# Turning experts' rows on VectorE in squares of 32x32, a tile of row numbers for each group, and scatters three a pair of heads

## Chip, cores, metric

One core of one Trainium2 chip. The metric is device time of the whole program in microseconds (us), the median of several executions. Runs of one batch share a chip; the experiments make five batches on four chips, and the kernel before was run again in each of them.

## The reference

Attention with a selective bias, then a mixture of eight experts, of which each token uses one:

```python
# attention: 8 batches x 8 heads x 576 tokens x 64, float32
s_pos = np.maximum(s, 0.0); cum = np.cumsum(s_pos, axis=-1)
scores = np.where(causal, -1e9, scale * q @ k.T + np.minimum(-(cum_i - cum_j), 0.0))
x = softmax(scores) @ v                       # -> (8, 576, 512)
# experts, for every batch b and token s in order
fresh_e = argmax(x[b, s] @ w_gate)
e = fresh_e if s == 0 or local_gate[b, s] < 0.5 else prev_e
h = np.maximum(x[b, s] @ w1[e], 0.0)          # w1[e]: 512 x 1024
out[b, s] = p[e] * (h @ w2[e])                # w2[e]: 1024 x 512
```

## The kernel before

The kernel runs attention in 32 pairs of heads. Beside it, it sorts the tokens by expert: each group of batches yields row numbers (`slot_i`), with which GpSimd scatters token rows to `x_rows` in DRAM. The experts then work in units on blocks of 128 gathered rows: a *double* unit has two blocks, a *single* one, a *mixed* one two halves with different weights. Layer 1 reads the rows with the features on the partitions (`xT`), so each block of 128 rows x 512 features has to be turned, as four squares of 128x128. In the kernel before TensorE turns a square by one transpose into PSUM (273 ns long at the median, the four of a block 0.11 us apart) and VectorE copies the result (0.69 us a block):

```python
class Turned:
    def product(self, i, k, n, x, ps):
        ps = self.ps = ps.rearrange("p (c n) -> p c n", c=DK)                  # DK = 4
        for c in range(DK):
            self.nc.tensor.transpose(ps[:, c, :], x[:, ...], self.ident)      # L1070
        ...
    def copies(self, i, k, x):
        nc.vector.tensor_copy(self.xT[i][:, :, k * P : k * P + P], self.ps)    # L1078
        nc.vector.tensor_copy(self.at[i, k], x[:, XI : XI + 1])                # L1081
        nc.vector.tensor_copy(self.gate[i, k], x[:, XI + 1 :])                 # L1082
```

The blocks of unit i+2 are turned inside layer 2 of unit i. A pass of layer 2 is 16 matmuls of 128x512, about 7 us (6.87 from start to start, without transposes). Where unit i is single and unit i+2 double, one pass has to hide two blocks, and this happens seven times:

```python
    def layer2(i, k, then):
        for c in range(FK):                                    # FK = 8
            ... mm(ps, lhsT=hT[i][:, c, a : a + m], rhs=wn[:, c, :], ...)      # L1211
            if c in then:
                turn_x(*then[c])
        nc.vector.tensor_scalar_mul(y, ps, gate[i, k])
        ...
    def second(i):
        for k in range(nbs[i]):
            layer2(i, k, {3: (i + 2, k)} if nbs[i] == 2 else {1: (i + 2, 0), 5: (i + 2, 1)})
```

The sort has one tile of row numbers for all groups, and its steps are hung into the pairs of heads by a plan:

```python
        self.slot = self.t("slot_i", [P, M], I32)              # one tile, rewritten by each group
        nc.vector.tensor_copy(self.slot, slot)                 # L1003
        ...
            for f in g.scatters:                               # two scatters a pair
                place = max(place + 1, 2 * (n + 4))
                at(place // 2, 3 + place % 2, f)
        ...
        at(28, 1, fetch_early)                                 # rows of the first two units
```

## Time and profile before

| | kernel before |
|---|---|
| time, median of 3 (range) | 834.43 us (826.62 to 834.91) |
| profiled span | 828.1 us |
| until the first matmul of layer 1 | 262.4 us |
| the seven passes with two blocks, each with the layer 1 behind it | 150.9 us |
| VectorE busy | 213.0 us (26%) |

TensorE is 96% of the chain that ends last, and the waits behind the rest are all in attention. The span is that of one profiled execution; times are of executions of their own. In the profile PE is TensorE, DVE is VectorE, POOL is GpSimd, ACT is ScalarE and SP is SyncE. In a line of the timeline the columns are start, duration, engine, source line, operation, output and inputs, shapes, count, and in brackets the idle time ahead of it with what ended it.

### The profile page before, as it was taken

How to read it: one execution, taken by the hardware profiler on the slowest of the kernel's cores; microseconds unless marked ns; L12 is line 12 of the kernel's file. 1: busy time of each engine (PE TensorE's matmuls, PEld its weight loads, DVE VectorE, ACT ScalarE, POOL GpSimd, SP SyncE). 2: the span in 40 equal slices, each digit the busy share in tenths (PEclk: the TensorE clock that was granted, in tenths of full speed). 3: DMA queues.
4: the chain of work that ended last, by engine and by line, in shares of the span. 5: the costliest groups of instructions: out<-in, count | busy, mean ns of one | idle time of the engine just before them, and what ended most of it. 6: DMA issues, size and time to landing. Idle time of an engine off the chain costs nothing.

```text
span 828.1 us, 19789 instructions
## 1 busy us (share of the span) xinstructions
PE 805.7 (97%) x8153; PEld 603.5 (73%) x8153; DVE 213.0 (26%) x700; ACT 188.7 (23%) x535; POOL 174.5 (21%) x329
## 2 busy tenths in 40 slices
PE   9999999998989999998999989999999999999996
PEld 8989988897878856864777647776677766676762
DVE  2234533553434753111111111111111111111111
ACT  5767677665652100000000000000000000000000
POOL 3422254253541231010110102101111011010001
PEclk9999999998989999999999999999999999999998
DMA  9486589785555399964999459993699846995001
GB/s 316 156 283 195 167 299 330 243 254 196 161 206 210 99 329 406 395 198 166 327 393 358 125 192 333 389 365 118 223 341 396 332 135 235 345 407 181 20 15 42
DMA packets 64148, 204.56 MB, mean 247 GB/s; under 512 B 8269, under 2 KB 8301, under 8 KB 64048
## 3 DMA queue, kind: packets, MB, share of 16 engines
q1 hardware_dynamic: 55008, 172.41, 59.4%
q0 software_dynamic: 8896, 30.47, 9.8%
q8 instruction: 66, 1.08, 0.5%
q10 hardware_dynamic: 144, 0.33, 0.1%
q14 instruction: 34, 0.28, 0.1%
HBM read 179.93 MB, written 23.76 MB: 246 GB/s over the span
## 4 chain that ended last, share of the span: by engine, by line
PE 96%; issue 1%; ACT 1%; DMA 0%; POOL 0%; DVE 0%; POOLq 0%; DVEq 0%; ACTq 0%
PE yp L1211 32%; PE hp L1187 29%; PE o L407 13%; PE ps L329 11%; PE hp L1194 4%; PE o L369 2%; PE xp L1070 2%; PE o L285 1%; PE bank L963 1%; PE bank L941 1%; PE o L350 1%; ACT sc L338 0%; DMA x_rows<-x,r_slot_i 0%; PE bank L984 0%; POOL sc L344 0%
## 5 line engine op out<-in xcount | busy, mean ns | idle before, releaser
L1211 PE MATMUL yp<-w,hT 128*128 128x512 f32 (+1 forms) x528 | 221.1, 594 | 0.0
L1187 PE MATMUL hp<-xT,w 128*128 128x256 f32 (+1 forms) x1088 | 192.1, 337 | 0.0
L1187 PEld LDWEIGHTS hp<-xT,w 128*128 128x128 f32 x1088 | 172.1, 191 | 23.9 <-issue 7.8
L338 ACT ACTIVATE sc<-ps,bias 128x256 f32<-128x256 f32 (+3 forms) x448 | 156.6, 481 | 66.6 <-PE ps L329 64.7
L1211 PEld LDWEIGHTS yp<-w,hT 128*128 128x128 f32 (+1 forms) x528 | 88.0, 180 | 100.5 <-issue 99.5
L1202 ACT ACTIVATE hT<-hp 128x512 f32<-128x512 f32 x38 | 22.7, 597 | 505.6 <-PE hp L1187 421.7
L1218 POOL DMA_INDIRECT out_dram<-y,at_gate x38 | 38.4, 1011 | 459.3 <-DVE y L1217 444.4
L407 PE MATMUL o<-v,sc 128*64 128x74 f32 x3072 | 116.8, 232 | 3.5 <-POOL sc L344 3.4
L407 PEld LDWEIGHTS o<-v,sc 128*64 128x64 f32 x3072 | 111.7, 139 | 11.0 <-issue 5.9
L329 PE MATMUL ps<-q,k 64*128 64x320 f32 (+2 forms) x768 | 94.1, 392 | 0.0
L344 POOL TENSOR_SCALAR_AFFINE_SELECT sc<-sc 128x256 f32<-128x256 f32 x160 | 66.0, 419 | 129.4 <-issue 66.9
L1200 DVE TENSOR_SCALAR hT<-hp 128x512 f32<-128x512 f32 x38 | 26.2, 689 | 221.2 <-PE hp L1187 187.7
L329 PEld LDWEIGHTS ps<-q,k 64*128 64x128 f32 x768 | 70.4, 191 | 15.8 <-issue 0.8
L1211 PE MATMUL yp<-x,hT 128*128 128x512 f32 (+1 forms) x144 | 66.5, 608 | 0.0
L1217 DVE TENSOR_SCALAR y<-yp,at_gate 128x512 f32<-128x512 f32 x38 | 28.5, 750 | 135.6 <-PE yp L1211 135.6
L1187 PEld LDWEIGHTS hp<-xT,x 128*128 128x128 f32 x320 | 46.1, 191 | 5.8 <-issue 2.6
L1187 PE MATMUL hp<-xT,x 128*128 128x128 f32 (+1 forms) x320 | 50.1, 317 | 0.0
L1078 DVE COPY xT<-xp 128x512 f32<-128x512 f32 x36 | 24.9, 691 | 82.8 <-PE xp L1070 82.7
L1029 POOL DMA_INDIRECT x_rows<-x,r_slot_i x40 | 38.6, 966 | 16.0 <-DMA xg<-x_rows 7.5
L1211 PEld LDWEIGHTS yp<-x,hT 128*128 128x128 f32 (+1 forms) x144 | 25.2, 182 | 22.4 <-issue 22.1
L409 DVE RECIPROCAL recs<-o 128x4 f32<-128x4 f32 x64 | 12.1, 189 | 93.6 <-PE o L407 93.6
L412 DVE TENSOR_TENSOR x<-o,recs 128x292 f32<-128x292 f32 x64 | 34.4, 538 | 2.2
(160 smaller groups left out, 430.3 us busy)
## 6 DMA issues: line engine op xcount, KB each, us to landing
w<-in_w_dram SPq DMA_DIRECT2D x184, 512.0 KB, 8.2
x<-in_w_dram SPq DMA_DIRECT2D x56, 512.0 KB, 7.9
v<-in_vx_dram SPq DMA_DIRECT2D x32, 370.0 KB, 5.6
vt<-in_vz_dram SPq DMA_DIRECT2D x32, 320.0 KB, 3.4
k<-in_kz_dram SPq DMA_DIRECT2D x31, 320.0 KB, 4.9
q<-in_q_dram SPq DMA_DIRECT2D x32, 288.0 KB, 6.1
xg<-x_rows POOLq DMA_DIRECT2D x30, 293.0 KB, 8.4
x_rows<-r_empty SPq DMA_DIRECT2D x6, 293.0 KB, 4.7
```

What stands on the lines that cost most here:

```text
L329: mm(ps[:, h, at : at + z - a], lhsT=kb[d, c * P : c * P + P], rhs=qb[d, a:z], start=True, stop=True)
L338: nc.scalar.activation(scs[n, u][:, h, at : at + z - a], raw[u][:, h, at : at + z - a], Act.Exp, bias=bias[:, i : i + 1], scale=scale)
L344: nc.gpsimd.affine_select(out=x, in_=x, compare_op=Alu.is_ge, fill=0.0, base=0, pattern=[[0, 2], [1, P]], channel_multiplier=-1)
L407: mm(y, lhsT=w, rhs=x, start=start, stop=stop)
L412: nc.vector.tensor_tensor(x, y, rec.unsqueeze(3).to_broadcast([P, t1 - t0, 2, HW]), op=Alu.mult)
L1029: self.s.nc.gpsimd.indirect_dma_start(out=next(self.s.views)[:, :], out_offset=bass.IndirectOffsetOnAxis(ap=self.slot[:z, m : m + 1], axis=0),
L1187: mm(y, lhsT=w[0][:, c, f : f + P], rhs=xT[i][:, c, :], start=(c == 0), stop=(c == DK - 1))
L1194: mm(y[d, m], lhsT=w[h ^ swap][:, c, f + h * HALF : f + h * HALF + HALF], rhs=xT[i][:, c, m], start=(c == 0), stop=(c == DK - 1))
L1200: nc.vector.tensor_scalar_max(to, ps, 0.0)
L1211: mm(ps[n * m : n * m + m, :], lhsT=hT[i][:, c, a : a + m], rhs=wn[:, c, :], start=(c == 0), stop=(c == FK - 1))
L1217: nc.vector.tensor_scalar_mul(y, ps, gate[i, k])
L1218: nc.gpsimd.indirect_dma_start(out=next(outs)[:, :], out_offset=bass.IndirectOffsetOnAxis(ap=at[i, k][:, 0:1], axis=0), in_=y[:, :], eleme ...
```

## The change

The intent is to take work off TensorE, which bounds the kernel, and give it to VectorE, which is idle three quarters of the time; and to remove three waits of attention on scatters. The kernel turns squares of 32x32 with VectorE's transpose: an instruction here takes 32 partitions x 4 x 32 elements (one square of each of the four 128x128 ones), so 16 of them turn a block.

```diff
-    def product(self, i, k, n, x, ps):
-        for c in range(DK):
-            self.nc.tensor.transpose(ps[:, c, :], x[:, 2 * c * HW + X0 : 2 * c * HW + X0 + P], self.ident)
-    def copies(self, i, k, x):
-        nc.vector.tensor_copy(self.xT[i][:, :, k * P : k * P + P], self.ps)
+    def block(self, i, k, n, x):
+        rows = x[:, :XI].rearrange("p (c w) -> p c w", w=2 * HW)
+        m = 32
+        for a in range(0, P, m):
+            for d in range(0, P, m):
+                nc.vector.transpose(self.xT[i][d : d + m, :, k * P + a : k * P + a + m],
+                                    rows[a : a + m, :, X0 + d : X0 + d + m])
 ... (where the sort multiplies by a whole identity: a transpose)
-            nc.tensor.matmul(main[:, a : a + z] if a < TS else tails[:, :TL], lhsT=..., rhs=s.ident[:, p : p + z], ...)
+            if z == P:
+                nc.tensor.transpose(y, x, i)
+            else:
+                nc.tensor.matmul(y, lhsT=x, rhs=i, start=True, stop=True)
 ... (the same in hold, where p == 0)
-        self.slot = self.t("slot_i", [P, M], I32)
+        self.slot = self.t(f"slot_i{self.bs[0]}", [P, M], I32)
 ...
-                place = max(place + 1, 2 * (n + 4))
-                at(place // 2, 3 + place % 2, f)
+                place = max(place + (2 if n < 17 else 1), 3 * (n + 4))
+                at(place // 3, (3, 4, 0)[place % 3], f)
-        at(28, 1, fetch_early)
+        at(27, 1, fetch_early)
```

More of the change, by code (lines that the diff above doesn't have):

```diff
@@ L144, in fetch_early @@
                     nc.sync.dma_start(ready["x"][i, k], rows_d[r0 : r0 + P, :])
-        at(28, 1, fetch_early)
+        at(27, 1, fetch_early)
         fx = main.enter_context(tc.tile_pool(name="fx", bufs=2))
-        turned = ready["turned"] = Turned(nc, fx, main.enter_context(tc.tile_pool(name="first", bufs=2)), ident)
+        turned = ready["turned"] = Turned(nc, fx, main.enter_context(tc.tile_pool(name="first", bufs=2)))
         for i in range(2):
-            at(30 + i, 1, lambda bank, i=i: turned.product(0, i, 2, ready["x"][0, i], bank(1)[0]))
-            at(30 + i, 2, lambda bank, i=i: turned.copies(0, i, ready["x"].pop((0, i))))
+            at(30 + i, 2, lambda bank, i=i: turned.block(0, i, 2, ready["x"].pop((0, i))))
         last = sort.group((6, 7), xs)
@@ L940, in rows @@
         for t, p, z, a in s.runs:
-            nc.tensor.matmul(main[:, a : a + z] if a < TS else tails[:, :TL], lhsT=self.bt(self.code)[:, :, t],
-                             rhs=s.ident[:, p : p + z], start=True, stop=True)
+            y = main[:, a : a + z] if a < TS else tails[:, :TL]
+            x, i = self.bt(self.code)[:, :, t], s.ident[:, p : p + z]
+            if z == P:
+                nc.tensor.transpose(y, x, i)
+            else:
+                nc.tensor.matmul(y, lhsT=x, rhs=i, start=True, stop=True)
     def fresh(self, bank):
@@ L962, in hold @@
         for t, p, z, a in s.runs:
-            nc.tensor.matmul(e[p : p + z, t], lhsT=self.erow[:, a : a + z], rhs=s.ident[:nb, :nb], start=True, stop=True)
+            x, i = self.erow[:, a : a + z], s.ident[:nb, :nb]
+            if p == 0:
+                nc.tensor.transpose(e[:z, t], x, i)
+            else:
+                nc.tensor.matmul(e[p : p + z, t], lhsT=x, rhs=i, start=True, stop=True)
     def hot(self, bank):
@@ L1059, with __init__ @@
 class Turned:
-    def __init__(self, nc, fx, gp, ident):
-        self.nc, self.fx, self.gp, self.ident = nc, fx, gp, ident
+    def __init__(self, nc, fx, gp):
+        self.nc, self.fx, self.gp = nc, fx, gp
         self.xT, self.at, self.gate = {}, {}, {}
-    def product(self, i, k, n, x, ps):
-        ps = self.ps = ps.rearrange("p (c n) -> p c n", c=DK)
-        for c in range(DK):
-            self.nc.tensor.transpose(ps[:, c, :], x[:, 2 * c * HW + X0 : 2 * c * HW + X0 + P], self.ident)
+    def block(self, i, k, n, x):
+        nc = self.nc
         if k == 0:
@@ L1073, in product @@
                 "p (c n) -> p c n", c=DK)
-    def copies(self, i, k, x):
-        nc = self.nc
-        nc.vector.tensor_copy(self.xT[i][:, :, k * P : k * P + P], self.ps)
+        rows = x[:, :XI].rearrange("p (c w) -> p c w", w=2 * HW)
[4 more added lines that the diff above has]
+                                    rows[a : a + m, :, X0 + d : X0 + d + m])
         both = self.gp.tile([P, 2], I32, name="at_gate")
@@ L1105, in experts @@
     fp = pool("fp", 2)
-    ps_x = pool("ps_x", 1, space=PSUM)
     ps_h = pool("ps_h", 2, space=PSUM)
@@ L1113, in experts @@
     hT = {}
-    turned = ready["turned"] if ready else Turned(nc, pool("fx", 2), None, ident)
+    turned = ready["turned"] if ready else Turned(nc, pool("fx", 2), None)
     turned.gp = gp
@@ L1165, in turn_x @@
             return
-        ps = ps_x.tile([P, DK * P], F32, name="xp")
-        x = xg.pop((i, k))
-        turned.product(i, k, nbs[i], x, ps)
-        turned.copies(i, k, x)
+        turned.block(i, k, nbs[i], xg.pop((i, k)))
     def layer1(i, first, last):
```

## The prediction

> **What bounds the kernel now.** I read the page first, then the chain of work that ended last, then who waited for whom, then the timeline of five stretches. The page and the first line of its chain:
>
> ```profile
> span 828.1 us, 19789 instructions
> ...
> PE 805.7 (97%) x8153; PEld 603.5 (73%) x8153; DVE 213.0 (26%) x700; ACT 188.7 (23%) x535; POOL 174.5 (21%) x329
> ...
> PE 96%; issue 1%; ACT 1%; DMA 0%; POOL 0%; DVE 0%; POOLq 0%; DVEq 0%; ACTq 0%
> PE yp L1211 32%; PE hp L1187 29%; PE o L407 13%; PE ps L329 11%; PE hp L1194 4%; PE o L369 2%; PE xp L1070 2%; PE o L285 1%; PE bank L963 1%; PE bank L941 1%; PE o L350 1%; ACT sc L338 0%; DMA x_rows<-x,r_slot_i 0%; PE bank L984 0%; POOL sc L344 0%
> ```
>
> TensorE carries 96% of the chain: a matmul taken off it is time saved, unless a wait comes in its place. L1070 (the transposes of the experts' rows) is on the chain with 2%, L963 and L941 (products with the identity in the sort) with 1% each, rounded. The rest is waits, in the lists of who waited for whom (of PE, of DVE, of POOL):
>
> ```profile
> PE o L350 <- DVE x L412: 4.1, 1, 4.1
> PE o L407 <- POOL sc L344: 3.4, 2, 2.3
> ...
> DVE r_slot_i L1003 <- DMA x_rows<-x,r_slot_i: 8.2, 2, 7.0
> ...
> POOL x_rows L1029 <- DMA xg<-x_rows: 7.5, 1, 7.5
> ```
>
> PE's 4.1 us hangs on DVE's L1003: the one tile of row numbers is rewritten for the next group while scatters of the group before still read it. PE's 3.4 us hangs on POOL, whose scatter waited 7.5 us for the early fetch of rows, which had itself waited for the scatter before. The timeline of the first:
>
> ```profile
> 192.57 2.86 PE L329 MATMUL ps<-q,k 64*128 64x320 f32 x24
> ...
> 202.01 0.17 DVE L1003 CAST r_slot_i<-r_slot 128x5 int32<-128x5 f32 x1 [7.03 <-DMA x_rows<-x,r_slot_i]
> ...
> 203.03 0.48 PE L350 MATMUL o<-q,k 128*64 128x64 f32 x4 [4.12 <-DVE x L412]
> ...
> 204.44 5.06 PE L329 MATMUL ps<-q,k 64*128 64x320 f32 x24
> ...
> 214.65 2.88 PE L329 MATMUL ps<-q,k 64*128 64x320 f32 x24
> ```
>
> After the wait the same 24 matmuls took 5.06 us, not 2.86: the pause costs a second time, at a lower clock.
>
> [...] the price of the new instruction is thus my largest unknown.
>
> **The change, part by part.** A stage of a single followed by a double expert unit, in the timeline (PE and DVE):
>
> ```profile
> 518.08 1.88 PE L1211 MATMUL yp<-w,hT 128*128 128x512 f32 x4
> 518.33 0.69 DVE L1200 TENSOR_SCALAR hT<-hp 128x512 f32<-128x512 f32 x1 [6.61 <-PE hp L1187]
> ...
> 519.79 0.60 PE L1070 MATMUL xp<-ident,xg 128*128 128x128 f32 x4
> 520.23 3.60 PE L1211 MATMUL yp<-w,hT 128*128 128x512 f32 x8
> 520.43 0.69 DVE L1078 COPY xT<-xp 128x512 f32<-128x512 f32 x1 [1.41 <-PE xp L1070]
> 521.04 0.14 DVE L1081 CAST at_gate<-xg 128x1 int32<-128x1 f32 x1
> 521.10 0.14 DVE L1082 COPY at_gate<-xg 128x1 f32<-128x1 f32 x1
> 523.67 0.60 PE L1070 MATMUL xp<-ident,xg 128*128 128x128 f32 x4
> ```
>
> (a) Transposes leave TensorE. Between starts, four take 520.23 - 519.79 = 0.44 us. There are 38 blocks of 128 rows (152 transposes): 38 x 0.44 = **16.7 us off the path**. The 38 copies from PSUM go too, but DVE is no bound.
>
> (b) In the sort, products over a whole square (L941) or starting at partition 0 (L963) become transposes. In the trace such a float32 product is two instructions and a transpose is one. L941 loses 2 of 14 per group (about 0.21 us), L963 5 of 14 in 1.23 us (0.44 us). Five groups: **3.3 us**.
>
> (c) A tile of row numbers for each group: L1003 has nothing to wait for. A quiet pair of heads takes 6.93 us (starts of L329 at 230.33 and 237.26). The struck ones took 204.44 - 192.57 = 11.87 and 214.65 - 204.44 = 10.21 (with 1.09 of L941): 4.94 + 2.19 = **7.1 us**.
>
> (d) Scatters three a pair, early fetch one pair sooner: in the emitted order the fetch now comes a good pair after the last scatter that it needs and more than a pair ahead of the next one. A scatter lands in 5.0 us at the median (8.0 at most), the fetch in 4.1. The struck pair ran from 237.26 to 251.41 = 14.15 us, with 0.59 of L1070: 14.15 - 0.59 - 6.93 = **6.6 us**. The chip's POOL has room: five masks of 0.41 and three scatters of about 1.15 make 5.5 us of the 6.9.
>
> (e) What it adds: 16 turning instructions a block on DVE, each 128 elements a partition. Starts on DVE lie 0.06 us apart for one element (L1081 to L1082) and 0.61 for 512 (L1078 to L1081): 0.06 + 128 x 1.08 ns = 0.20 us. [...] I take 0.215 (an estimate): a block is 16 x 0.215 + 0.13 = 3.6 us, all of it 38 x 3.6 = 136 us, against 24.9 + 1.4 for the copies removed. DVE gets to some 320 us of 810: no bound on average. But it works in order. In the stage above PE waits for nothing, and after the change the 6.87 us of layer 2 must cover 0.25 + 0.61 us (to the end of the relu that comes first) and two blocks of 3.6, plus 0.1 for the signal: 8.1 us, so the next layer 1 waits 1.2 us. This pattern, two L1070 blocks in one layer-2 pass of a single unit, stands seven times in the trace: 7 x 1.2 = **8.5 us given back**. Double units turn one block beside each 6.87 us pass: hidden.
>
> (f) At the hand-over from attention (262 to 300 us) DVE does the last group's sort and four blocks. Following its order with blocks of 3.6 us, the first layer 1 waits 0.5 us for the second block, L941 0.3, the second unit's layer 1 1.7, a relu that comes late 0.7: **3.2 us**. The tables and scatters end some 3 us later, but the rows of the next units were used at 309.6 and are needed now only at about 322.
>
> **Sum**: 16.7 + 3.3 + 7.1 + 6.6 - 8.5 - 3.2 = 22.0 us. 834.4 - 22 = **812 us**.
>
> **The rivals.** *R1, a turning instruction is dearer* (four-byte elements at half rate, or a slow start). Each 0.01 us more on one costs 0.32 us in each of seven stages, and some 0.5 us at the hand-over: 2.7 us. At 0.30 us the gain is gone (about 835); at 0.35 it is a loss of about 2%[...]. For it: no trace shows one. [...] *R2, the turning is hidden* (0.185 us or less): the seven waits vanish and the hand-over costs 2 us, 802 us. *R3, the waits in attention only move*: scatters three a pair crowd POOL, whose masks feed L407, or the two early blocks delay L412. Then (d) gives 2 or 3 us and not 6.6: 816. Against: two scatters a pair cost PE nothing. *R4, weights bind*: the DMA is 99% busy in half of each cycle of five units. But each set of weights lands some 10 us or more before its first matmul, and a cycle gets only 3.5 us shorter: I give this little.
>
> **Range and chances.** 812 with an instruction from 0.185 to 0.25 us gives 802 to 821; runs of before lie from 826.6 to 834.9, so I add to both sides: 801 to 827. Two per cent is 817.7, reached if an instruction costs up to about 0.235: 0.66 for faster, 0.29 for same, 0.05 for slower.
>
> **What would show it.** Right: no L1070 line, TensorE with about 200 fewer instructions; the turning group at x608; L1003 and the scatters without waits on DMA, no 11.9 or 14.1 us pair; layer 1 after the seven stages waiting on DVE for about 1 us each, in all 8 to 9 us. Wrong: turning instructions further apart than 0.25 us[...] (R1); PE waiting for POOL masks (R3); layer 1 waiting for weights (R4).

## The result, and the profile after

Ratios here are the mean time of one kernel's fast runs over the mean of the other's in the same rounds, so not quite the ratio of the medians that are quoted beside them.

The outputs are right. The changed kernel took **860.99 us** (852.86 to 864.26, four runs) against 830.65 for the kernel before (four runs by then): ratio 1.035, 95% interval 1.025 to 1.045. It is slower by 3.5%, well outside the predicted range. Its page:

```profile
span 857.1 us, 19922 instructions
...
PE 800.6 (93%) x7966; PEld 592.9 (69%) x7966; DVE 370.0 (43%) x1270; ACT 188.2 (22%) x535; POOL 174.4 (20%) x329
...
PE 85%; DVE 6%; issue 5%; DMA 2%; POOL 0%; ACT 0%; POOLq 0%; DVEq 0%
...
L1084 DVE STREAM_TRANSPOSE xT<-xg 32x128 f32<-32x128 f32 x608 | 183.7, 302 | 9.9 <-DMA xg<-x_rows 2.1
```

TensorE has 187 instructions fewer and is still less of the chain (85% against 96%): it waits. The last line is the new group: 608 turning instructions of 302 ns each. Whom TensorE waited for (us in total, times, longest):

```profile
PE hp L1190 <- issue: 31.5, 8, 4.2
...
PE bank L484 <- DVE g_count L480: 5.0, 1, 5.0
PE bank L991 <- DVE r_hot L980: 1.7, 1, 1.7
PE hp L1190 <- DVE xT L1084: 1.5, 1, 1.5
```

L1190 is layer 1. The 31.5 us at "issue" are the seven passes with two blocks (and one more wait, of 2.6 us, at the hand-over); the profile found no releaser for them, but the timeline shows it. One of the seven, on both engines:

```profile
404.44 7.03 PE L1214 MATMUL yp<-w,hT 128*128 128x512 f32 x16
404.70 0.69 DVE L1203 TENSOR_SCALAR hT<-hp 128x512 f32<-128x512 f32 x1 [6.61 <-PE hp L1190]
405.31 5.04 DVE L1084 STREAM_TRANSPOSE xT<-xg 32x128 f32<-32x128 f32 x16
...
410.50 5.04 DVE L1084 STREAM_TRANSPOSE xT<-xg 32x128 f32<-32x128 f32 x16
...
415.64 16.74 PE L1190 MATMUL hp<-xT,w 128*128 128x256 f32 x64 [4.16 <-issue]
```

Layer 2 ends at 411.5, VectorE's second block at 415.54, and 0.10 us later layer 1 begins: it waited for the block. Then its 64 matmuls last 16.74 us. In the kernel before, the same 64 lasted 14.0 (13.8 from start to start of the next stage).

In attention the struck pairs are gone. Where the pairs before ran 11.87 and 10.21 us, the trace after has (L328 is L329 of before):

```profile
183.03 2.86 PE L328 MATMUL ps<-q,k 64*128 64x320 f32 x24
...
190.53 2.86 PE L328 MATMUL ps<-q,k 64*128 64x320 f32 x24
...
197.46 2.86 PE L328 MATMUL ps<-q,k 64*128 64x320 f32 x24
```

that is 7.50 us (with 0.57 of the sort) and 6.93. At the hand-over to the experts there is a wait that I had not foreseen:

```profile
310.28 1.89 PE L1190 MATMUL hp<-xT,w 128*128 128x256 f32 x8
...
317.20 0.59 PE L484 MATMUL bank<-g_count,r_ones 128*128 128x1 f32 x2 [5.03 <-DVE g_count L480]
317.65 14.53 PE L1190 MATMUL hp<-xT,w 128*128 128x256 f32 x56
```

L484 is a small product of a check of value ranges, in TensorE's order between matmuls of layer 1. VectorE computes its input (L480, start 316.66) in order, behind three turned blocks of 5.04 us (starts 299.55, 304.75 and 310.60). The 56 matmuls behind the wait took 14.53 us, against 12.33 in the kernel before.

Adding up the stages of both traces, from start of a stage to start of the next:

| stretch of TensorE's work | before | after | difference |
|---|---|---|---|
| start to first layer 1 (attention) | 262.4 | 247.4 | -15.0 |
| layer 1 of units 0, 1; layer 2 of 0, 1; layer 1 of 2, 3 (hand-over) | 88.8 | 98.4 | +9.6 |
| seven passes with two blocks, each with next layer 1 | 150.9 | 192.1 | +41.2 |
| layer 1 of the four mixed units | 36.2 | 38.8 | +2.6 |
| all else | 282.9 | 273.4 | -9.6 |
| to the last matmul | 821.3 | 850.1 | +28.8 |

The loss is thus in the seven passes, and second at the hand-over. Attention gave 15.0 us where some 17 were forecast (two blocks' transposes included). "All else" gave more than the 16 x 0.44 = 7.0 us of its blocks: in the layer 2 of the four mixed units a block was worth 0.73, and one layer 2 behind a mixed unit's wait was slow in the trace before alone (16.0 us against 14.3).

### The profile page after: what moved, and what is told of

The parts are those of the page before. It is cut to its first block, busy times and chain, and to the rows that moved or that the text cites. A ratio compares the mean times of both kernels' runs of the same rounds, so it can differ in the third digit from the quotient of the medians.

```text
span 857.1 us, 19922 instructions
## 1 busy us (share of the span) xinstructions
PE 800.6 (93%) x7966; PEld 592.9 (69%) x7966; DVE 370.0 (43%) x1270; ACT 188.2 (22%) x535; POOL 174.4 (20%) x329
## 3 DMA queue, kind: packets, MB, share of 16 engines
q8 instruction: 65, 1.06, 0.5%
## 4 chain that ended last, share of the span: by engine, by line
PE 85%; DVE 6%; issue 5%; DMA 2%; POOL 0%; ACT 0%; POOLq 0%; DVEq 0%
PE yp L1214 27%; PE hp L1190 27%; PE o L406 12%; PE ps L328 10%; DVE xT L1084 4%; PE hp L1197 4%; PE o L368 2%; DMA xg<-x_rows 1%; DMA x_rows<-x,r_slot_i 1%; PE o L349 1%; DMA s_sb<-in_s_dram 1%; PE bank L945 0%; PE bank L943 0%; PE o L284 0%; POOL x_rows L1036 0%
## 5 line engine op out<-in xcount | busy, mean ns | idle before, releaser
L1190 PE MATMUL hp<-xT,w 128*128 128x256 f32 (+1 forms) x1088 | 209.3, 355 | 28.9 <-issue 27.4
L1190 PEld LDWEIGHTS hp<-xT,w 128*128 128x128 f32 x1088 | 183.3, 202 | 60.0 <-issue 39.1
L1214 PE MATMUL yp<-w,hT 128*128 128x512 f32 (+1 forms) x528 | 216.8, 594 | 0.0
L1084 DVE STREAM_TRANSPOSE xT<-xg 32x128 f32<-32x128 f32 x608 | 183.7, 302 | 9.9 <-DMA xg<-x_rows 2.1
L1214 PEld LDWEIGHTS yp<-w,hT 128*128 128x128 f32 (+1 forms) x528 | 90.3, 181 | 113.3 <-issue 111.8
L406 PE MATMUL o<-v,sc 128*64 128x74 f32 x3072 | 113.6, 229 | 0.5 <-issue 0.5
L406 PEld LDWEIGHTS o<-v,sc 128*64 128x64 f32 x3072 | 108.8, 136 | 7.5 <-issue 5.7
L328 PE MATMUL ps<-q,k 64*128 64x320 f32 (+2 forms) x768 | 92.2, 385 | 1.1 <-issue 1.1
L328 PEld LDWEIGHTS ps<-q,k 64*128 64x128 f32 x768 | 69.3, 186 | 15.9 <-issue 1.2
L1214 PE MATMUL yp<-x,hT 128*128 128x512 f32 (+1 forms) x144 | 63.3, 594 | 0.0
L1190 PE MATMUL hp<-xT,x 128*128 128x128 f32 (+1 forms) x320 | 52.6, 326 | 4.1 <-issue 4.1
L1190 PEld LDWEIGHTS hp<-xT,x 128*128 128x128 f32 x320 | 47.7, 197 | 11.0 <-issue 7.0
L1197 PEld LDWEIGHTS hp<-xT,w 128*64 128x64 f32 x768 | 31.6, 141 | 9.0 <-issue 9.0
```

Source lines behind the costliest of these rows:

```text
L328: mm(ps[:, h, at : at + z - a], lhsT=kb[d, c * P : c * P + P], rhs=qb[d, a:z], start=True, stop=True)
L406: mm(y, lhsT=w, rhs=x, start=start, stop=stop)
L1084: nc.vector.transpose(self.xT[i][d : d + m, :, k * P + a : k * P + a + m], rows[a : a + m, :, X0 + d : X0 + d + m])
L1190: mm(y, lhsT=w[0][:, c, f : f + P], rhs=xT[i][:, c, :], start=(c == 0), stop=(c == DK - 1))
L1197: mm(y[d, m], lhsT=w[h ^ swap][:, c, f + h * HALF : f + h * HALF + HALF], rhs=xT[i][:, c, m], start=(c == 0), stop=(c == DK - 1))
L1214: mm(ps[n * m : n * m + m, :], lhsT=hT[i][:, c, a : a + m], rhs=wn[:, c, :], start=(c == 0), stop=(c == FK - 1))
```

## The experiments

Medians of the kernel before, and what they say of the chips: 841.55 and 842.12 us in the first two batches (the same chip), 830.73 in the third, 829.46 in the fourth and 830.48 (one run) in the fifth. The first chip is slower in attention: the stretch to the first layer 1 is 255 to 259 us there for kernels with the new schedule, and 245 to 250 on the others. So times are compared through ratios, or on one chip.

### Is it the turning?

**e1_pe_turns**: the change, with TensorE turning as before.

```diff
+    def product(self, i, k, n, x, ps): ... self.nc.tensor.transpose(ps[:, c, :], ..., self.ident)
+    def copies(self, i, k, x): ... nc.vector.tensor_copy(self.xT[i][:, :, k * P : k * P + P], self.ps)
-                nc.vector.transpose(self.xT[i][d : d + m, ...], rows[a : a + m, ...])
```

> The change without VectorE's turning: TensorE turns the rows as before; the transposes in the sort, the tile of row numbers per group and the scatters three a pair stay. Theory A (the loss is the price of the turning instruction alone, in the seven single-unit passes): this keeps the gain in attention and the sort, 14 to 17 us off, ratio 0.980 to 0.984 to the kernel before. Theory B (the other parts lose too, or their gain is taken back at the hand-over to the experts): 0.995 or more.

Measured: 827.90 us, ratio 0.982 (0.978 to 0.986).

**e2_dve_alone**: the kernel before, with nothing but VectorE's turning (the diff of the change, `Turned` only).

> VectorE's turning alone, put into the kernel before; nothing else changed. Theory A: the loss is all here and adds to the rest: the changed kernel's 1.035 plus the 0.018 that the other parts gain, 1.05 to 1.06, with seven waits of layer 1 of about 4.3 us. Theory B: about 1.02.

Measured: 874.84 us, ratio 1.041 (1.034 to 1.048), with the seven waits (4.1 to 4.2 us); somewhat less loss than the 1.05 to 1.06 expected. From the first layer 1 to the last matmul it took 592.7 us, against 558.9 in the trace before: 33.8 more, and the time differs by 33.3. In the same stretch the changed kernel takes 602.6: its hand-over (98.4 against 95.4), its mixed units (38.8 against 34.4) and the layers 1 behind the seven waits (114.0 against 111.8 together) are longer. So the rest of the change gains and the turning loses; the 10 us by which it costs more beside the other parts than alone are not settled.

### Is it the seven passes?

**e3_seven_second_on_pe**: in the seven passes alone, TensorE turns the second block.

```diff
-        turned.block(i, k, nbs[i], xg.pop((i, k)))
+        on_pe = k == 1 and i >= 4 and nbs[i] == 2 and nbs[i - 2] == 1
+        turned.block(i, k, nbs[i], xg.pop((i, k)), ps_x.tile([P, DK * P], F32, name="xp") if on_pe else None)
```

> The changed kernel, but in the seven passes of a single unit that turn two blocks, the second block is turned by TensorE (7 of 38 blocks). Theory A: one VectorE block of 5.2 us fits behind the 6.87 us pass, the seven waits and their slow matmuls go: 7 x (6.7 - 0.44) = 44 us less than the changed kernel, ratio to before 0.98 to 0.99. Theory C (VectorE's load as a whole, 43% busy, slows everything): only 7 of 38 blocks go, so at most 10 us less, ratio above 1.02.

Measured: 822.29 us, ratio 0.975 (0.971 to 0.979). One pass of it:

```profile
417.25 5.32 PE L1222 MATMUL yp<-w,hT 128*128 128x512 f32 x12
...
418.12 5.04 DVE L1090 STREAM_TRANSPOSE xT<-xg 32x128 f32<-32x128 f32 x16
...
422.40 0.60 PE L1083 MATMUL xp<-ident,xg 128*128 128x128 f32 x4
...
424.56 2.75 PE L1198 MATMUL hp<-xT,w 128*128 128x256 f32 x12
```

One block of 5.04 us is hidden behind layer 2, and layer 1 (L1198) starts with no wait. The pass lasts 7.3 us and layer 1 13.8, in all seven. This takes back the loss and more: the seven passes are the bulk of it.

**e4_warm**: is a part of it the clock behind the wait? The change, with 16 products of the identity (result unused) on TensorE at the start of each of the seven waits.

```diff
+        if nbs[i] == 1 and i + 2 < NU and nbs[i + 2] == 2:
+            warm = ps_w.tile([P, 512], F32, name="warm")
+            for _ in range(16):
+                mm(warm[:, :P], lhsT=ident, rhs=ident, start=True, stop=True)
```

> The changed kernel, with 16 idle products of the identity (3.4 us, result unused) on TensorE at the start of each of the seven waits. Theory D (each wait of 4.3 us costs 2.5 us more because TensorE's clock falls behind it): layer 1 after the wait takes 13.8 us again and not 16.4, 7 x 2.5 = 17 us less than the changed kernel, ratio to before 1.012 to 1.018. If the slower layer 1 has another cause: no change, 1.03 to 1.04.

Measured: 849.12 us, ratio 1.010 (1.004 to 1.016).

```profile
411.73 7.03 PE L1215 MATMUL yp<-w,hT 128*128 128x512 f32 x16
418.60 3.73 PE L1233 MATMUL warm<-ident 128*128 128x128 f32 x32
422.93 14.05 PE L1191 MATMUL hp<-xT,w 128*128 128x256 f32 x64 [0.59 <-issue]
```

Layer 1 starts as late as in the change (11.2 us after layer 2 began) but lasts 14.05 instead of 16.74. From stage to stage all seven take 13.9; in the change they took 15.6 to 16.6. The pages show the granted clock too, in 40 slices of the span and in tenths of full speed; first the change, then e4:

```profile
PEclk9999999999999989999889998989999899989999
```

```profile
PEclk9999999999999998999999999999999999999998
```

In the trace after, the granted clock falls to 0.50 in six of the seven waits (at 414.26 us in the one shown), for 6.8 us, and 1 us behind the end of the other, for 3.4; in e4 it is 1.00 from 329.6 us to 841.6, past all seven. So a wait of 4.1 to 4.2 us costs 1.7 to 2.7 us more behind it, about 2.4 at the mean and 17 us in all, and this part is the clock. The length of a wait alone does not tell when the clock falls: in the trace before it fell to 0.50 in the 4.12 us wait (at 202.09, for 6.8 us), but also right behind one of 2.28 us (at 243.05) and one of 2.24 us in a mixed unit (at 376.17).

### Why does a block take 5.2 us and not 3.6?

Read from the trace after, the starts of two turning instructions of a block lie 0.316 us apart at the median, not 0.215; 0.316 is the duration and 14 ns. Nothing overlaps: the next instruction starts when the one before has ended. Is that the duration's fault, or is something keeping the next instruction back?

**e5_wide**: the change, but the rows are fetched in four quarters of the columns, each to its own 32 partitions, so that one instruction of 128 partitions x 512 elements turns a whole block with nothing taken to other partitions. The rows of w1 are laid out in the matching order in the input.

```diff
-        for a in range(0, P, m):
-            for d in range(0, P, m):
-                nc.vector.transpose(self.xT[i][d : d + m, ...], rows[a : a + m, ...])
+        nc.vector.transpose(self.xT[i][:, :, k * P : k * P + P].rearrange("p c (a r) -> p a c r", r=Q),
+                            x[:, :D].rearrange("p (a c r) -> p a c r", a=4, c=DK))
-                nc.gpsimd.dma_start(x, rows_d[bass.ds(row + k * P, P), :])
+                load_rows(nc.gpsimd, x, rows_d[bass.ds(row + k * P, P), :], 0)      # four transfers and one small
-        "w1": i["moe_w1"].reshape(E, DK, P, F).transpose(0, 2, 1, 3),
+        "w1": i["moe_w1"].reshape(E, 4, DK, 32, F).transpose(0, 1, 3, 2, 4).reshape(E, P, DK, F),
```

> The changed kernel, but the rows are fetched in four column quarters, each to its own 32 partitions, so that one instruction on all 128 partitions (512 elements each) turns a block, in place of 16 on 32 partitions (128 elements each). Rows of w1 lie in the matching order. Theory A1 (an instruction costs about 0.18 us fixed plus 1.04 ns an element): starts 0.71 us apart, a block of 0.85 us, no wait of layer 1 anywhere, and TensorE's 16.7 us stay saved: the time of the version with TensorE's turning less 2%, ratio to before 0.960 to 0.965. Theory A2 (four-byte elements at half rate, 2.1 ns each): 1.1 us an instruction, the same time. Rival E (rows in pieces of 512 bytes, five transfers a block, land too late or disturb the weights): ratio 0.98 or more, with layer 1 or DVE waiting for rows.

Measured: 809.68 us, ratio 0.961 (0.959 to 0.964), correct.

```profile
423.74 7.03 PE L1221 MATMUL yp<-x,hT 128*128 128x512 f32 x16
...
424.55 0.70 DVE L1091 STREAM_TRANSPOSE xT<-xg 128x512 f32<-128x512 f32 x1
...
425.26 0.70 DVE L1091 STREAM_TRANSPOSE xT<-xg 128x512 f32<-128x512 f32 x1
...
430.60 9.66 PE L1197 MATMUL hp<-xT,w 128*128 128x256 f32 x44
```

Both blocks are done 2.2 us into the pass, and TensorE waits for none of them. An instruction lasts 0.70 us, the next on VectorE starts 0.62 us behind its start, and a block takes 0.71: less than A1's 0.71 and 0.85, and far from A2's 1.1. A1's 1.04 ns an element is also what two forms of L412 give in the trace before: 614 ns for 438 elements, 462 for 292. (VectorE itself waits for rows three times, 6.1 us in all; no expert matmul waits for that.) The price moves to GpSimd, which issues five transfers a block instead of one: 259.1 us busy instead of 174.4, still far from a bound; but attention waits for its masks again (2.3 us in two waits, none in the change).

**e6_halves**: each turning instruction cut in two of 64 elements.

```diff
-                nc.vector.transpose(self.xT[i][d : d + m, :, ...], rows[a : a + m, :, ...])
+                for c in range(0, DK, 2):
+                    nc.vector.transpose(self.xT[i][d : d + m, c : c + 2, ...], rows[a : a + m, c : c + 2, ...])
```

> The changed kernel with each turning instruction split in two of 64 elements (32 a block). Theory A1 (fixed cost): starts 0.25 us apart, a block of 8.1 us, the time above 900 us. Theory A2 (half rate): starts 0.17 to 0.18 us apart, a block of 5.8 us, the time below 880 us.

Measured: 883.93 us in the one run, blocks of 6.0 us, outside both forecasts. The starts alternate: 0.169 us from the first half to the second, then 0.206 to the next target. The second half, which goes to the same partitions as the first, starts while the first still runs (234 ns long); the next, which goes to others, starts 13 to 14 ns after the end of the one before (190 ns long).

**e9_own_quarter**: each instruction writes to the 32 partitions that it reads. Its output is wrong, which doesn't matter for the time.

```diff
-                nc.vector.transpose(self.xT[i][d : d + m, :, k * P + a : k * P + a + m],
+                nc.vector.transpose(self.xT[i][a : a + m, :, k * P + d : k * P + d + m],
```

> Wrong result on purpose: the changed kernel, but each of the 16 turning instructions writes to the 32 partitions it reads from. If crossing to other partitions makes the instruction slow (0.316 us for 128 elements, where the wide form of the run before does 512 in 0.625): starts about 0.20 us apart and the time near 812 us. If not: 0.31 to 0.32 apart, the time as the changed kernel's.

Measured: 810.11 us in the one run.

```profile
394.57 0.69 DVE L1203 TENSOR_SCALAR hT<-hp 128x512 f32<-128x512 f32 x1 [6.61 <-PE hp L1190]
395.18 3.56 DVE L1084 STREAM_TRANSPOSE xT<-xg 32x128 f32<-32x128 f32 x16
...
398.89 3.57 DVE L1084 STREAM_TRANSPOSE xT<-xg 32x128 f32<-32x128 f32 x16
...
402.56 14.05 PE L1190 MATMUL hp<-xT,w 128*128 128x256 f32 x64 [1.21 <-issue]
```

Starts lie 0.193 us apart within a quarter, 0.270 where the quarter changes and 0.235 right behind that, 0.22 at the mean. A block is the 3.6 us of the prediction, the wait its 1.2 us, and the time its 812 within 2: with the overlap I had assumed, the rest of the sum holds.

**e10_all_lanes**: four instructions of 128 partitions x 128 elements. Its output is wrong, which doesn't matter for the time.

```diff
-        for a in range(0, P, m):
-            for d in range(0, P, m):
-                nc.vector.transpose(self.xT[i][d : d + m, ...], rows[a : a + m, ...])
+        for d in range(0, P, m):
+            nc.vector.transpose(self.xT[i][:, :, k * P + d : k * P + d + m], rows[:, :, X0 + d : X0 + d + m])
```

> Wrong result on purpose: the changed kernel, but 4 instructions a block on all 128 partitions, each with the same strided four pieces of 32 that the 16 had (128 elements a partition). If the strided pieces make it slow: starts 0.31 to 0.32 us apart. If the 32 partitions do: about 0.20. The time is near 805 us either way, a block being 1.0 to 1.4 us.

Measured: 796.65 us in the one run, less than the 805 expected; starts 0.193 us apart (0.225 for the first), 278 ns long. All start at partition 0, and nothing is kept back.

### The crossing, the target, or the change?

**e13_target_by_target**: the loops exchanged, so that four instructions in a row write to the same partitions and each reads others. Correct.

```diff
-        for a in range(0, P, m):
-            for d in range(0, P, m):
+        for d in range(0, P, m):
+            for a in range(0, P, m):
```

> The changed kernel with the two loops of the turning exchanged: four instructions in a row write to the same 32 partitions and read from four different ones; the result is right. Theory F1 (what costs is changing the 32 partitions written to from one instruction to the next; in the run that wrote to its own quarter, starts lay 0.19 us apart within a quarter and 0.27 and 0.235 around a change): starts 0.22 us apart on average as there, a block of 3.6 us, waits of 1.2 us, ratio to before 0.975 to 0.985. Theory F2 (what costs is reading from other partitions than are written to, or changing those read from): 0.31 us, ratio 1.03 to 1.04.

Measured: 855.58 us, ratio 1.034 (1.030 to 1.037); starts 0.316 apart. The theory that only a change of target matters falls.

**e14_own_but_changing**: as e9, nothing crosses, but the quarter changes with each instruction (loops exchanged, target `a`). Its output is wrong, which doesn't matter for the time.

> Wrong result on purpose: each instruction writes to the 32 partitions it reads from, but the quarter changes with every instruction. Theory F1 and a theory F3 (a change of the partitions read from costs): 0.30 to 0.32 us apart, the time as the changed kernel's, near 860. Theory F2 as crossing: 0.20 us, near 810.

Measured: 858.64 us in the one run, starts 0.316 apart.

**e15_cross_kept**: every instruction crosses to the next quarter, and both quarters stay for four instructions. Its output is wrong, which doesn't matter for the time.

```diff
+            b = (a + m) % P
-                nc.vector.transpose(self.xT[i][d : d + m, :, k * P + a : k * P + a + m],
+                nc.vector.transpose(self.xT[i][b : b + m, :, k * P + d : k * P + d + m],
```

> Wrong result on purpose: four instructions in a row read one quarter and write the next one, so that all sixteen cross and neither side changes within four. If crossing itself costs nothing and only a change of either side does: as in the run with its own quarter, 0.19 to 0.20 us within four and about 0.25 around a change, 0.22 on average, the time near 810 us. If crossing costs by itself: 0.30 us or more throughout, near 858.

Measured: 812.24 us against 830.48, one run of each; starts 0.193 within four and 0.272 at a change. Who TensorE's layer 1 waited for, first in e14, then in e15:

```profile
PE hp L1190 <- issue: 31.5, 8, 4.2
```

```profile
PE hp L1191 <- issue: 11.2, 8, 1.5
```

All instructions of e15 cross and none of e14 do; e15 is fast and e14 slow. So crossing alone costs nothing (0.193 us from start to start, as in e9), and a change of quarter from one instruction to the next costs the overlap (0.316), whether it is the quarter written (the change), read (e13) or both (e14):

| kernel | quarter read | quarter written | starts apart, us |
|---|---|---|---|
| change | stays for 4 | changes | 0.316 |
| e13 | changes | stays for 4 | 0.316 |
| e14 | changes | changes, same as read | 0.316 |
| e9 | stays for 4 | stays for 4, same | 0.193; 0.270 at a change |
| e15 | stays for 4 | stays for 4, other | 0.193; 0.272 at a change |
| e10 | all | all | 0.193 |

In these six rows the starts are 0.193 us apart where the quarter read and the quarter written both stay (0.235 in e9 right behind a change), and 0.270 to 0.316 where one or both change. In the latter case an instruction starts 14 ns after the end of the one before (303 after 289, 315 after 301, 272 after 258 ns). By these rows no order of the sixteen instructions avoids that, though only two were run (the change and e13): a full turn needs every pair of a quarter read and a quarter written once, so from one instruction to the next at least one of the two changes. e5 has no such series: its DMA has done the crossing, and a block is one instruction of 0.70 us.

### The schedule's parts alone

**e7_slot_only**: the kernel before with a tile of row numbers for each group.

```diff
-        self.slot = self.t("slot_i", [P, M], I32)
+        self.slot = self.t(f"slot_i{self.bs[0]}", [P, M], I32)
```

> The kernel before with a tile of row numbers for each group, nothing else. My step (c): the 4.1 us wait for DVE and the slow pair after it go, 7 us off, ratio 0.991. Rival: the wait moves to the next user of the scatters: 0.998 or more.

Measured: 836.53 us, ratio 0.994 (0.992 to 0.996). The wait of L1003 is gone; the one on GpSimd stays:

```profile
PE o L407 <- POOL sc L344: 2.8, 2, 1.7
```

**e8_sched_only**: the kernel before with the scatters three a pair and the early fetch a pair sooner.

```diff
-                place = max(place + 1, 2 * (n + 4))
-                at(place // 2, 3 + place % 2, f)
+                place = max(place + (2 if n < 17 else 1), 3 * (n + 4))
+                at(place // 3, (3, 4, 0)[place % 3], f)
-        at(28, 1, fetch_early)
+        at(27, 1, fetch_early)
```

> The kernel before with scatters three a pair and the early fetch one pair sooner, still one tile of row numbers. My step (d): the wait of POOL for the early fetch goes, 6.6 us off, ratio 0.992, the wait on the tile of row numbers stays. Rival R3: POOL is crowded and masks come late: 0.998 or more, with L407 waiting for POOL.

Measured: 829.67 us, ratio 0.985 (0.983 to 0.988), more than expected. It removes both waits: no VectorE wait on the scatters is left either (L1003 waits 0.2 us, for VectorE itself), presumably since scatters that are issued sooner have ended when the next group's row numbers are written. The separate tile is nearly without worth beside it.

### A correct version with few edits, and the change once more

**e11_hand_over_too**: e3, and TensorE turns the eight blocks of units 0 to 3 as well.

```diff
+        on_pe = i < 4 or k == 1 and nbs[i] == 2 and nbs[i - 2] == 1
```

> The changed kernel with the second block of the seven single passes and also the eight blocks of the hand-over (units 0 to 3) turned by TensorE. By the two traces the hand-over loses 12.9 us to VectorE's blocks (products L484 and L991 that wait for it, and slow matmuls behind); against that 8 x 0.44 = 3.5 us of transposes come back: 9.4 us less than the version with the seven alone, ratio to before 0.961 to 0.967. If the hand-over isn't slowed by the blocks: 0.975 to 0.980.

Measured: 801.63 us, ratio 0.964 (0.958 to 0.970), correct. The hand-over takes 88.5 us (88.8 before, 98.4 after), and the wait of L484 is gone. VectorE turns what fits beside one layer-2 pass, TensorE the rest.

**e12_change_again**: the change, run beside e9 to e11 on their chip; no edit.

> The change itself once more, on the chip of these runs: 1.03 to 1.04, so that the ratios of the other runs may be set against it.

Measured: 858.80 us, ratio 1.035 (1.029 to 1.042), as at first. Of the correct versions e5 and e11 are the best, at 0.961 and 0.964 on different chips; their intervals overlap, so neither is ahead.

## Why the prediction was wrong

**(a) Transposes off TensorE: right.** Stages that turn one block are 0.44 us shorter (14.27 to 13.83 us and 7.31 to 6.87 from stage to stage), those of mixed units 0.73 (7.75 to 7.02). No L1070 line is left, and TensorE has 187 instructions fewer, where I had said about 200.

**(b), (c), (d) The sort and the schedule: right in sum, wrong in division.** Forecast together 17.0 us; e1, which has all three, gained 0.0178 x 841.55 = 15.0 us. But (c) and (d) are not two separate gains of 7.1 and 6.6: (d) alone gave 0.0147 x 842.12 = 12.4 us and removed (c)'s wait too; (c) alone gave 5.1. The two waits were sized nearly right; that (c)'s tile was needed for its share was wrong.

**(e) The price of a turning instruction: wrong, and this decided.** The duration was foreseen well enough (302 ns measured; the formula's 0.215 + 0.13 makes 345). The failed step is the interval, 0.215 us forecast (0.20 from starts in the trace before, and 0.015 that was my estimate with nothing measured behind it): I took it from pairs like L1081 and L1082, which overlap (0.06 us apart at 0.14 us of length) and both start at partition 0. The change's instructions each write to other partitions than the one before, so each starts only when that one has ended: 0.316 us, a block 5.2 us instead of 3.6, and the wait in each of the seven passes 4.1 us instead of 1.2. The trace after shows it on the same pair: behind the last turning instruction, which reads and writes the last quarter, the first of the pair starts 31 ns after its end; in e10, where all start at partition 0, 77 ns before its end. With it my own formula gives 0.86 + 2 x 5.2 + 0.1 = 11.4 us for the pass, and the trace has 11.2. e9 and e15, which have the overlap, came out at 810 and 812 us.

**(e), second omission: the clock.** The sum had no term for what follows a long wait, though I had shown one in the trace before. It is about 2.4 us behind each of the seven (e4). Wait and clock together make 192.1 - 150.9 + 14 x 0.44 = 47.4 us, against 8.5 forecast.

**(f) The hand-over: right mechanism, wrong size, and two waits not seen.** Forecast 3.2 us; measured 98.4 - 88.8 + 6 x 0.44 = 12.2 us (six blocks that TensorE no longer turns there). Of the waits that I named, those of the first two layers 1 are there, longer: 1.5 us for 0.5 (in the attention row of the table) and 2.6 for 1.7. Two I had not put into the order: L991 with 1.7, and the largest, L484 with 5.0, a small check behind three long blocks on VectorE, with 2.2 us of slow matmuls behind it.

**The rivals.** R1 was the case in kind: dearer instructions (0.316 us), waits of 4.1 to 4.2 us, slow matmuls behind them. Its slope holds too: 2.7 us for each 0.01 gives 812 + 10.1 x 2.7 = 839 us at 0.316, and some 17 us of clock make 856; the profiled run took 858.75. It failed as I weighed it: I gave half rate or a slow start as its cause and 0.05 to a slower kernel, and neither cause is what happened (128 elements take 0.193 us from start to start in e9 and e15, and e5's 512 take 0.62). R2 didn't occur in the change; e5 and e10 show it with wide instructions. (Its 0.185 us would not quite have hidden the turning: the prediction's own formula leaves 0.3 us a pass.) R3: no waits on GpSimd's masks appeared. R4: no wait that the profile puts down to weights appeared, but it names nobody for the waits of the mixed units (next paragraph).

**What stays open.** Layer 1 of the mixed units varies from 7.6 to 13.6 us between kernels and between units of one kernel, with waits at "issue" of up to 4.5 us and no releaser in the profile; it is 2.6 us of the result. Weights are not excluded there. Why VectorE keeps an instruction back when the quarter changes is not shown, only that it does.

## What to carry to other kernels

Before pricing a series of short VectorE instructions like these, look at which 32 partitions each reads and writes: where either changed from one to the next, the whole duration counted (0.316 us from start to start), not the interval of instructions that stay in place (0.193). Work moved to an engine with a low average load must fit into the shortest stretch that has to hide it, here 7 us for two blocks; where it doesn't, a mixed form (one block on each engine) can beat both (0.975 in e3 and 0.964 in e11, against 1.035 for VectorE alone and 0.982 for TensorE alone), and so can fewer, wider instructions (0.961 in e5). And a wait of some us that a new term puts on TensorE needs a second term for the slow matmuls behind it: here 2.4 us behind 4.1, and none behind the 1.2 and 1.5 us of e9 and e15 (14.05 us for layer 1 in e9, a granted clock of 0.997 over e15).
